# Decode attention, forward and backward over one KV cache: which cache blocks stay in SBUF between the four passes, and V turned in place at the end of the second pass

## The chip, the cores and the metric

The kernel runs on one core of a Trainium2 chip. The metric is device time in microseconds (us) from the start to the end of one execution, as a median over several. The core has TensorE (PE, matmuls and transposes by matmul), VectorE (DVE), ScalarE (ACT), GpSimd (POOL), SyncE (SP, which here issues every load), 16 DMA engines, the on-chip memories SBUF and PSUM, and HBM, which holds the inputs and outputs.

## The reference

Two transformer layers for one new token are computed with the same weights and the same KV cache, and then the gradient of everything, by `jax.vjp`:

```python
def A(x):      # attention, 32 query heads, 4 KV heads of 65536 keys x 128
    q = (x @ wq).reshape(32, 128)
    s = einsum("hd,hkd->hk", q, k) * 128 ** -0.5
    return (einsum("hk,hkd->hd", softmax(s), v)).reshape(4096) @ wo
def B(x):      # dense, squared relu, 1024 -> 3584 -> 1024
    return relu(x @ w1 + b1) ** 2 @ w2 + b2
x1 = x  + A(layernorm(x));   x2 = x1 + B(layernorm(x1))
x3 = x2 + A(layernorm(x2));  x4 = x3 + B(layernorm(x3))
outputs: x4 and the gradients of x, k, v, wq, wo, w1, b1, w2, b2
```

K and V have 4 groups x 65536 rows x 128 numbers in bf16: 64 MB (MiB) each, much more than SBUF holds. Each must be read again for every attention pass over it.

## The kernel before

**Four passes.** The cache is swept four times: p=0 is the forward attention of the first layer, p=1 that of the second, p=2 the backward pass of the second layer as far as it needs V and K for the gradient of q, p=3 the backward pass of both layers that also writes the gradients of K and V. Between them stand dense stages (`dense12` between p=0 and p=1, `dense23`, `dense34`), which stream the weights wo, w1, w2, wq.

**Steps.** A pass is a software pipeline of 256 items, each a group g (0 to 3) and 8 chunks of 128 rows; the 32 chunks that make a *block* of 1 MB in SBUF are four consecutive steps. A group has 16 blocks; K12 below is block 12 of the group at hand. In p=0 and p=1 (`attn_fwd`) an item goes through `kT` (lag 0: 8 transposes of K on PE into PSUM, one copy of 128x1024 on DVE or ACT back to SBUF), `kS` (lag 2: 8 matmuls for the scores) and `v8` (lag FWD_LAG: 8 matmuls for the output). Between `kS` and `v8` lie a chain of small steps (maximum, `turn`, `spread`, then the exponentials of a unit of 16 steps on ACT, line 996). In p=2 (`attn_bwd3`) V is transposed first (`vT`, lag 0; `vS`, lag 2) and K is read with lag 13 (`k8`); p=3 (`attn_bwd4`) does the same with blocks in falling order and K at lag 7, and stages its results, 1 MB per block, in SBUF before POOL issues the stores. The order on PE, DVE and ACT is the program's order in p=0 to p=2 (`manual_schedule`, lines 1059 and 1157); in p=3 the framework's scheduler sets it.

**Orders.** p=0 goes up through groups and blocks, p=1 goes down by units of 4 blocks but up inside a unit (first K12, K13, K14, K15, then K8 to K11 of group 3), p=2 goes up, p=3 goes down block by block.

**Slots.** All loads, kept blocks and staged results share an arena of 20 slots of 1 MB (`ARENA`, lines 240 to 246). Eight of them turn into planes for the exponentials as the passes go on (`hold`), so that 15 are left in the tail of p=0 and 12 from the end of p=1 on. `kv8` (line 320) loads a block, or two at once as 2 MB, where the program first touches it; `take_one` picks the slot. SP issues the loads in program order: it runs ahead of the engines until a load's slot is not yet free, and then everything behind that load waits too, the weights of the next dense stage among them.

**Keeping.** At the end of a pass up to `NKEEP` = 8, 7, 7 blocks are not given back but stay for the next pass. `TOUCH[p]` lists the blocks of a pass by first touch. `plan_keep` (line 382) takes, of the last NKEEP+2 blocks touched in pass p, those that the next pass touches first. That gives: after p=0, K15, V12, V13, V14, V15, V8, V9, V10 of group 3; after p=1, V0 to V6 of group 0; after p=2, K12, K13, K14, K15, V13, V14, V15 of group 3.

**Turned blocks.** A kept block whose transpose the pass makes anyway is overwritten by its transpose (`turned_to`, line 338: K in p=0, V in p=2). The next pass then skips `kT` or the 8 transposes and the copy of `vT` for it (`is_turned`). In p=1 K is what is transposed and V is what is kept, so nothing is turned there.

Of the kernel before, what the change touches and what calls it, by code (L numbers as in the profile page):

```python
# [20 lines left out]
def kernel(  # L21
# [24 lines left out]
    nc = tc.nc  # L46
# [10 lines left out]
    J = 32  # L57
    NB = C // J
    SU = min(128, C)
# [6 lines left out]
    TLEAD = 2  # L66
# [4 lines left out]
    NKEEP = [8, 7, 7]  # L71
# [16 lines left out]
    def ps_tr(shape=None, dtype=BF):  # L88
        return PS["pool"].tile(shape or [P, 8, P], dtype, name="ps_tr", tag="tr", bufs=2 if PS["pass4"] else 3)
# [7 lines left out]
    def ps_acc(shape):  # L97
        return PS["pool"].tile(shape, F32, name="ps_acc", tag="acc", bufs=1)
# [12 lines left out]
    ident_b = const.tile([P, P], BF, name="ident_b")  # L111
# [27 lines left out]
    def evac(out, in_, kind="bf"):  # L139
        n = 1  # L140
        for d in in_.shape[1:]:
            n *= d
        ca = 0.17 + n * 0.00083
        cd = 0.13 + n * (0.00105 if kind == "f32" else 0.00054)

        if PS["pass4"] and kind == "bf":
            ca += 1.5
        if kind == "kta" or kind != "kt" and load["act"] + ca <= load["dve"] + cd:
            load["act"] += 0.17 + n * 0.00083
            nc.scalar.copy(out=out, in_=in_)  # L150
        else:
            load["dve"] += cd
            nc.vector.tensor_copy(out=out, in_=in_)  # L153
# [161 lines left out]
    KV = {"have": {}, "keep": set(), "halves": set(), "turn": None, "turned": set()}  # L315
# [4 lines left out]
    def kv8(t, g, c8):  # L320
        hb, j = divmod(c8, J)
        key = (t, g, hb)
        have = KV["have"]
        if key not in have:
            i = None
            if NOW["pairs"] and hb % 2 == 0 and (t, g, hb + 1) not in have and key not in KV["halves"]:
                i = take_pair()
            if i is None:
                sl = Slot("blk_" + t, load=True)
                nc.sync.dma_start(out=sl.t.rearrange("p (j d) -> p j d", d=DH), in_=half(KVIN[t], g, hb))  # L330
                have[key] = sl
            else:
                for h in range(2):
                    have[(t, g, hb + h)] = Slot("blk_" + t, at=i + h)
                nc.sync.dma_start(out=wide(i).rearrange("p (j d) -> p j d", d=DH), in_=KVIN[t][g][hb // 2])
        return have[key].t.rearrange("p (j d) -> p j d", d=DH)[:, j:j + 8, :]
# [9 lines left out]
    def kv_done(t, g, c8):  # L346

        key = (t, g, c8 // J)
        if c8 % J == J - 8 and key not in KV["keep"]:
            KV["have"].pop(key).free()  # L350

    def order_by_unit(desc, unit):
        out = []
        gs = range(G)
        us = range(C // unit)
        for g in (reversed(gs) if desc else gs):
            for u in (reversed(us) if desc else us):
                out += [(g, c8) for c8 in range(u * unit, (u + 1) * unit, 8)]
        return out

    def touch_order(items, stages):
        seen, out = set(), []
        maxlag = max(l for _, l in stages)
        for i in range(len(items) + maxlag):
            for t, lag in stages:
                if 0 <= i - lag < len(items):
                    g, c8 = items[i - lag]
                    key = (t, g, c8 // J)
                    if key not in seen:
                        seen.add(key)  # L370
                        out.append(key)
        return out

    FWD_LAG = TLEAD + SU // 8 + 11
    B3_LAG = TLEAD + HB // 8 + 3
    B4_LAG = TLEAD + J // 8 + 1
    DV_LAG = TLEAD + 1
    ITEMS = [order_by_unit(False, SU), order_by_unit(True, SU), order_by_unit(False, HB), order_by_unit(True, J)]
    TOUCH = [touch_order(ITEMS[0], [("k", 0), ("v", FWD_LAG)]), touch_order(ITEMS[1], [("k", 0), ("v", FWD_LAG)]),
             touch_order(ITEMS[2], [("v", 0), ("k", B3_LAG)]), touch_order(ITEMS[3], [("v", 0), ("k", B4_LAG)])]  # L380

    def plan_keep(p):
        if p == 3:
            return set()
        last = TOUCH[p][-(NKEEP[p] + 2):]
        return set([k for k in TOUCH[p + 1] if k in last][:NKEEP[p]])

    def start_pass(p):  # L390
        KV["keep"] = plan_keep(p)
        KV["turned"] = KV.get("next", set())
        KV["next"] = set()
        KV["turn"] = {0: "k", 2: "v"}.get(p)
        NOW["pairs"] = p < 3
        KV["halves"] = set(TOUCH[p][-8:] + (TOUCH[p][:10] if p else []))
# [368 lines left out]
    def first_at(n, fn):  # L765
        TASKS.setdefault(NOW["i"] + n - 0.5, []).append(fn)
# [5 lines left out]
    def pipeline(items, stages, bg, end=(), holds=()):  # L772
        maxlag = max(l for _, l in stages)
        for i in range(len(items) + maxlag):
            NOW["i"] = i
            NOW["wide"] = NOW["pairs"]
            for at, k in holds:
                if i == at:
                    hold(k)
            tasks(i - 0.5)  # L780
            for n, (fn, lag) in enumerate(stages):
                if 0 <= i - lag < len(items):
                    fn(*items[i - lag])
                if n == 0:
                    tasks(i)
            bg.step(i)
            NOW["wide"] = False
            NOW["step"] += 1
            for before, fn in end:
                if i == len(items) + maxlag - before:  # L790
                    fn()
        while TASKS:
            k = min(TASKS)
            NOW["i"] = int(k + 0.5)
            tasks(k)
# [17 lines left out]
    def E(lay, g, c0, n):  # L813
        assert plane(lay, g) in HELD and plane(lay, g) not in BUSY
        return EALL[:, lay, g, c0:c0 + n, :]
# [73 lines left out]
    def attn_fwd(p, L, on_group, bg, end=()):  # L889
# [112 lines left out]
        def v8(g, c8):  # L1002
            su = c8 // SU
            vb8 = kv8("v", g, c8)
            if c8 % SU == 0:
                state["ps_o"] = ps_acc([P, 8, R])
            if c8 % SU == SU // 2 and su != first_su[g]:
                t = tmp.tile([P, R], F32, name="o_t")
                nc.vector.tensor_tensor(out=t[:], in0=state[("o", g)][:], in1=state[("al", g, su)][:], op=ALU.mult)
                state[("ot", g)] = t  # L1010
            ps_o = state["ps_o"]
            for i in range(8):
                c = c8 + i
                w = min(8, (su + 1) * SU - c)
                nc.tensor.matmul(ps_o[:, 0:w, :], lhsT=vb8[:, i, :], rhs=E(p, g, c, w),  # L1015
                                 start=(c % SU == 0), stop=(c % SU == SU - 1), skip_group_check=True)
            kv_done("v", g, c8)
            if (c8 + 8) % SU == 0:
                first_at(1, lambda: unit_end(g, su, ps_o))

        def unit_end(g, su, ps_o):
            on = spool.tile([P, R], F32, name="oacc", tag="oacc", bufs=3)
            rs = state.pop(("rs", g, su))
            if su == first_su[g]:
                nc.vector.tensor_copy(out=on[:], in_=ps_o[:, 0, :])
                z2 = rs
            else:
                al = state.pop(("al", g, su))
                nc.vector.tensor_tensor(out=on[:], in0=ps_o[:, 0, :], in1=state.pop(("ot", g))[:], op=ALU.add)
                zn = spool.tile([P, R], F32, name="zn", tag="zn")  # L1030
                nc.vector.tensor_tensor(out=zn[:], in0=state[("z", g)][:], in1=al[:], op=ALU.mult)
                z2 = spool.tile([P, R], F32, name="z2", tag="z2", bufs=3)
                nc.vector.tensor_tensor(out=z2[:], in0=zn[:], in1=rs[:], op=ALU.add)
            state[("o", g)] = on
            state[("z", g)] = z2
            if su == last_su[g]:
                after(2, lambda: group_sum(g, z2))
                after(3, lambda: group_out(g, su, on))
# [12 lines left out]
            nc.scalar.activation(out=L["fw"][:, g, :, :], in_=fd[:], func=ACTF.Exp)  # L1051

        start_pass(p)
        n = len(items) // G
        order = list(dict.fromkeys(g for g, _ in items))
        holds = [(k * n + 2, plane(p, g)) for k, g in enumerate(order) if k > 0]
# [2 lines left out]
        with tc.manual_schedule(engines=ORDERED):  # L1059
            pipeline(items, [(kT, 0), (kS, TLEAD), (v8, FWD_LAG)], bg, end, holds)  # L1060
        st.close()
# [381 lines left out]
    def on1(g):  # L1443
        if g != lastg[0]:
            bg.add(g_wo(L1, x1, g))
    attn_fwd(0, L1, on1, bg, [(10, pre_load("wo1", lambda: wo_slabs(lastg[0], 2)))])
    bg.drain()

# [190 lines left out]
```

## Time and profile before

| | |
|---|---|
| time, median of 4 runs | 2033.01 us (2031.31, 2032.86, 2033.15, 2041.23) |
| the profiled execution | 2041.23 us, span of the trace 2039.5 us |
| PE busy / DVE busy / ACT busy | 1656.6 / 1195.2 / 1048.3 us |
| bytes moved by DMA | 802.36 MB, 393 GB/s over the span |
| granted TensorE clock, mean | 0.896 of full speed |

One profiled execution is shown; it is the slowest of the four, 8.2 us above the median. A busy PE means that a matmul is in flight, not that the array is full. The tables by windows give, for each stretch of time, the busy time of each engine with its number of instructions, the granted clock, the share of time that the 16 DMA engines were busy (1.00 is all of it, rounding can give a little more) and the rate they moved.

By the first and last instructions of their lines, p=0 computes to 376 us, dense12 runs to about 427, p=1 to about 777, dense23 to 831, p=2 to 1198, dense34 to about 1250, p=3 to about 2015.

### The profile page before, as it was taken

The numbers are of one execution on the slowest core, as the hardware profiler recorded it, in microseconds if no ns is written. First come the engines' busy times: TensorE is split into PE (matmuls) and PEld (weight loads), VectorE is DVE, ScalarE is ACT, GpSimd is POOL, SyncE is SP. The second block draws the span as 40 slices with busy tenths as digits, with TensorE's granted clock in tenths as the row PEclk, the third lists the DMA queues.
The fourth block names the chain that finished last, engine by engine and source line by source line (L and its number), as shares of the span: only waits on it lengthen the run. The fifth ranks groups of instructions, "written<-read, shape, count | busy, mean of one in ns | idle before, by whom it ended". The sixth has DMA issues, their size and how long they took to land. (4 is left out here: it accounts for less than half of the span.)

```text
span 2039.5 us, 67934 instructions
## 1 busy us (share of the span) xinstructions
PE 1656.6 (81%) x30626; PEld 1364.1 (67%) x30626; DVE 1195.2 (59%) x2391; ACT 1048.3 (51%) x1620; POOL 144.2 (7%) x328
## 2 busy tenths in 40 slices
PE   6878788788887887877778788889788798698896
PEld 6878787788787776876667786555455455455554
DVE  5545464356554542535544457677658586677685
ACT  2434344244433433425444446777658585577575
POOL 0000000000000000000000001111112121111121
PEclk9989898699998986998998899989879897798898
DMA  9999999979999998899999996999999999999996
GB/s 389 424 416 419 421 422 412 358 299 389 419 419 415 418 414 313 343 419 413 424 416 419 414 364 236 419 424 422 416 408 409 359 423 403 371 408 423 424 376 254
DMA packets 112416, 802.36 MB, mean 393 GB/s; under 512 B 9584, under 2 KB 9598, under 8 KB 49534
## 3 DMA queue, kind: packets, MB, share of 16 engines
q1 hardware_dynamic: 88078, 632.33, 76.2%
q0 software_dynamic: 24048, 165.70, 19.6%
q8 instruction: 239, 3.92, 0.8%
q14 instruction: 51, 0.42, 0.1%
HBM read 632.30 MB, written 165.69 MB: 391 GB/s over the span
## 5 line engine op out<-in xcount | busy, mean ns | idle before, releaser
L153 DVE COPY kt<-ps_tr 128x1024 bf16<-128x1024 bf16 x809 | 555.5, 689 | 537.0 <-PE ps_tr L913 284.3
L150 ACT CAST arena<-ps_gg 128x1024 bf16<-128x1024 f32 (+2 forms) x455 | 442.6, 1009 | 200.3 <-PE ps_gg L1273 145.3
L913 PE MATMUL ps_tr<-ident_b,arena 128*128 128x128 bf16 x4064 | 332.3, 228 | 45.6 <-DMA arena<-in_A_k_cache_dram 31.4
L150 ACT COPY kt<-ps_tr 128x1024 bf16<-128x1024 bf16 x183 | 192.1, 1050 | 255.2 <-PE ps_tr L1098 160.1
L913 PEld LDWEIGHTS <-arena 128*128 128x128 bf16 x4064 | 251.0, 102 | 53.4 <-DMA arena<-in_A_k_cache_dram 34.7
L1015 PE MATMUL ps_acc<-arena 128*128 128x64 bf16 (+4 forms) x4096 | 212.6, 199 | 73.4 <-ACT arena L996 37.7
L153 DVE CAST arena<-ps_gg 128x1024 bf16<-128x1024 f32 (+2 forms) x188 | 225.0, 1197 | 65.7 <-PE ps_gg L1273 41.4
L1273 PE MATMUL ps_gg<-GG,xt 64*128 64x512 bf16 x1024 | 211.8, 412 | 40.1 <-DVE arena L153 20.7
L1219 PE MATMUL ps_tr<-ident_b,arena 128*128 128x128 bf16 x1952 | 188.8, 234 | 42.6 <-DMA arena<-in_A_v_cache_dram 40.9
L1015 PEld LDWEIGHTS <-arena 128*128 128x128 bf16 x4096 | 167.8, 103 | 76.2 <-issue 51.1
L931 PE MATMUL ps_sc<-L_qpad,kt 128*128 128x64 bf16 x4032 | 208.6, 196 | 7.0 <-issue 6.4
L1098 PE MATMUL ps_tr<-ident_b,arena 128*128 128x128 bf16 x2048 | 166.4, 227 | 39.8 <-DMA arena<-in_A_v_cache_dram 39.7
L1219 PEld LDWEIGHTS <-arena 128*128 128x128 bf16 x1952 | 127.3, 104 | 102.0 <-issue 55.9
L996 ACT ACTIVATE arena<-S_sb,L_negm 128x128 bf16<-128x128 f32 x256 | 164.5, 1002 | 49.9 <-DVE L_negm L981 49.9
L931 PEld LDWEIGHTS <-kt 128*128 128x128 bf16 x4032 | 175.7, 101 | 9.9 <-issue 6.6
L1098 PEld LDWEIGHTS <-arena 128*128 128x128 bf16 x2048 | 125.8, 102 | 43.8 <-DMA arena<-in_A_v_cache_dram 42.2
L1299 PE MATMUL ps_acc<-X,arena 128*128 128x64 bf16 (+3 forms) x2048 | 117.4, 198 | 13.4 <-DMA arena<-in_A_k_cache_dram 13.4
L996 ACT ACTIVATION_READ_ACCUMULATOR arena<-S_sb,L_negm 128x1 f32 x256 | 127.5, 498 | 0.0
L1252 PE MATMUL ps_sc<-DOB,kt 128*128 128x64 bf16 (+3 forms) x1952 | 125.1, 199 | 0.0
L1252 PEld LDWEIGHTS <-kt 128*128 128x128 bf16 x1952 | 90.7, 102 | 51.3 <-issue 50.0
L1299 PEld LDWEIGHTS <-arena 128*128 128x128 bf16 x2048 | 85.6, 101 | 45.9 <-issue 30.8
L1273 PEld LDWEIGHTS <-xt 64*128 64x128 bf16 x1024 | 61.1, 94 | 81.6 <-issue 42.3
(262 smaller groups left out, 2074.2 us busy)
## 6 DMA issues: line engine op xcount, KB each, us to landing
arena<-in_A_k_cache_dram SPq DMA_DIRECT2D x86, 2048.0 KB, 19.9
arena<-in_A_v_cache_dram SPq DMA_DIRECT2D x79, 2048.0 KB, 20.1
out_dram<-arena POOLq DMA_DIRECT2D x151, 1024.0 KB, 11.7
arena<-in_A_v_cache_dram SPq DMA_DIRECT2D x81, 1024.0 KB, 16.6
arena<-in_A_k_cache_dram SPq DMA_DIRECT2D x79, 1024.0 KB, 18.4
arena<-in_B_w_dram SPq DMA_DIRECT2D x32, 896.0 KB, 7.9
arena<-in_B_w_dram SPq DMA_DIRECT2D x21, 1024.0 KB, 9.9
arena<-in_A_wq_dram SPq DMA_DIRECT2D x20, 1024.0 KB, 16.2
```

Of the source, the lines that this page charges most:

```text
L150: nc.scalar.copy(out=out, in_=in_)
L153: nc.vector.tensor_copy(out=out, in_=in_)
L913: nc.tensor.transpose(pt[:, i, :], kb8[:, i, :], ident_b[:, :])
L931: nc.tensor.matmul(state["ps_s"][:, s:s + w, :].rearrange("p a b -> p (a b)"), lhsT=kt[:, i, :], rhs=L["qpad"][:, g, 0:w, :].rearrange("p ...
L996: nc.scalar.activation(out=E(p, g, c0, SU)[:, :, h], in_=S[:, h, :], func=ACTF.Exp, bias=L["negm"][:, g, su, h:h + 1], scale=SCALE, accum_ ...
L1015: nc.tensor.matmul(ps_o[:, 0:w, :], lhsT=vb8[:, i, :], rhs=E(p, g, c, w), start=(c % SU == 0), stop=(c % SU == SU - 1), skip_group_check=True)
L1098: nc.tensor.transpose(pt[:, i, :], vb8[:, i, :], ident_b[:, :])
L1219: nc.tensor.transpose(pt[:, i, :], vb8[:, i, :], ident_b[:, :])
L1252: nc.tensor.matmul(state["ps_dp"][:, s:s + w, :].rearrange("p a b -> p (a b)"), lhsT=vt[:, i, :], rhs=DOB[:, g, 0:w, :].rearrange("p a b - ...
L1273: nc.tensor.matmul(pg[:, 512 * h:512 * h + 512], lhsT=xt[64 * h:64 * h + 64, j1 // 8 + m, :], rhs=gg[64 * h:64 * h + 64, :, :].rearrange(" ...
L1299: nc.tensor.matmul(ps_dq[:, 0:w, :].rearrange("p a b -> p (a b)"), lhsT=kb8[:, i, :], rhs=X[:, s:s + w, :].rearrange("p a b -> p (a b)"), ...
```

## The change

```diff
-    FWD_LAG = TLEAD + SU // 8 + 11
+    FWD_LAG = TLEAD + SU // 8 + 12
...
     def plan_keep(p):
         if p == 3:
             return set()
-        last = TOUCH[p][-(NKEEP[p] + 2):]
-        return set([k for k in TOUCH[p + 1] if k in last][:NKEEP[p]])
+        return set([k for k in TOUCH[p + 1] if k[0] == "kvv"[p]][:NKEEP[p]])
...
             kv_done("v", g, c8)
+            if p == 1 and ("v", g, c8 // J) in early_turn:
+                pt = ps_tr()
+                for i in range(8):
+                    nc.tensor.transpose(pt[:, i, :], vb8[:, i, :], ident_b[:, :])
+                evac(vb8[:, :, :], pt[:, :, :], kind="kt" if c8 // 8 % 2 else "kta")
+                KV["next"].add(("v", g, c8))
...
         start_pass(p)
+        early_turn = set(k for k in TOUCH[p][:-2] if k in KV["keep"])
```

`plan_keep` now takes the first NKEEP blocks of one kind in the order of the next pass: K after p=0, V after p=1 and after p=2. That makes the kept sets K8 to K15 of group 3 after p=0 (one K and seven V before), V0 to V6 of group 0 after p=1 (the same set as before), V9 to V15 of group 3 after p=2 (three V and four K before). The number of kept blocks, and so the number of loads, is what it was. K kept in p=0 and V kept in p=2 are overwritten by their transposes through `turned_to`, which is unchanged.

In p=1, `v8` now transposes a kept V block right after its 8 matmuls and copies the result over the block, on DVE for every second item and on ACT for the others (`kind="kta"`). `early_turn` leaves out the last two blocks that p=1 touches, V2 and V3, so five blocks are turned: V0, V1, V4, V5, V6.

`FWD_LAG` is one step longer, 30 instead of 29 steps between `kT` and `v8`, in p=0 and in p=1.

## The prediction, made before the changed kernel was run

> **What bounds the kernel now.** I read the page's slices first, then windows of 5 us at the three dense stages, then PE's and SP's timelines there.
>
> ```profile
> DMA  9999999979999998899999996999999999999996
> GB/s 389 424 416 419 421 422 412 358 299 389 419 419 415 418 414 313 343 419 413 424 416 419 414 364 236 419 424 422 416 408 409 359 423 403 371 408 423 424 376 254
> ```
>
> Inside the passes the DMA engines are never free: 413 to 424 GB/s in most slices. At 420 GB/s a 1 MB block (1.049 MB decimal) costs 2.5 us. The bytes don't change with the edit, so inside a pass a faster engine is worth nothing. What can be won is DMA idle time, and that lies at the changes of pass: slices 8 and 9, 16 and 17, 24 and 25. There:
>
> ```profile
> core 0: us, PE busy (x) PEld busy (x) DVE busy (x) ACT busy (x) POOL busy (x), PEclk, DMA share, GB/s
> 425.00:462.50 37.50, 32.87 (x700) 32.22 (x701) 21.11 (x39) 12.42 (x25) 0.00 (x0) 0.91 0.60 228
> 775.00:795.00 20.00, 13.59 (x242) 13.03 (x242) 2.68 (x17) 1.77 (x3) 0.29 (x1) 0.64 0.65 239
> 840.00:860.00 20.00, 18.71 (x489) 17.95 (x486) 9.38 (x14) 7.35 (x8) 0.00 (x0) 1.00 0.71 258
> 1247.00:1270.00 23.00, 21.37 (x312) 13.85 (x310) 17.13 (x44) 14.15 (x16) 5.30 (x11) 0.85 0.26 104
> ```
>
> Against a share of 1.01 these are (1.01-0.60) x 37.5 = 15.4 us idle at the head of p=1, 7.2 us in the tail of p=1 and the layer norm behind it, 6.0 us at the head of p=2, 17.3 us at the head of p=3. The head of p=1 in detail, with SP's issues:
>
> ```profile
> 445.00:450.00 5.00, 4.45 (x108) 4.24 (x106) 3.81 (x8) 1.84 (x4) 0.00 (x0) 1.00 0.72 285
> 450.00:455.00 5.00, 1.80 (x45) 1.70 (x43) 1.37 (x2) 5.00 (x18) 0.00 (x0) 1.00 0.02 5
> 455.00:460.00 5.00, 5.00 (x103) 5.00 (x103) 1.97 (x3) 1.80 (x2) 0.00 (x0) 0.66 0.01 3
> ...
> 442.19 0.33 SPq L330 DMA_DIRECT2D arena<-in_A_v_cache_dram  x1
> 461.30 5.59 SPq L335 DMA_DIRECT2D arena<-in_A_k_cache_dram  x3
> ```
>
> Between 442 and 461 us SP issues nothing: seven slots hold V blocks that `v8` reads only from step 29 on, the rest hold K that is loaded and waits for its turn.
>
> **The change part by part.** The sum is made against the profiled execution (2041.2 us) and carried over to the median (2033.0) as a difference.
>
> *1. Head of p=1.* PE is rid of 28 groups of 8 transposes (7 more K blocks turned, 4 steps each). At full clock a step of `kT` and `kS` alone is 0.68 us apart, of which `kS` is 0.23:
>
> ```profile
> 440.67 0.35 PE L931 MATMUL ps_sc<-L_qpad,arena 128*128 128x64 bf16 x8
> 440.88 0.61 PE L913 MATMUL ps_tr<-ident_b,arena 128*128 128x128 bf16 x8
> 441.32 0.40 PE L931 MATMUL ps_sc<-L_qpad,kt 128*128 128x64 bf16 x8
> ```
>
> So a group of transposes costs PE 0.45 us. That is not the gain; the slots are. Before, nothing is given back until K blocks come in and are used. After, the first 32 steps of K need no load at all, so K12 can be used at once and frees its slot at step 5, K13 at 9, and so on, one per 4 steps. Following `take_one`, the loads stand in SP's order as wq, wq, V12, K4, V13, K5 (six slots that dense12's weights give back), V14-15 (K12 and K13's slots, step 9), K6-7 (step 17), V8-9 (step 25), K0-1 (step 33). From about 427 us the six keep the DMA busy 15 us, to 442, the three pairs 5 us each, to 457. Step 33 needs one chain of exponentials: some 7 us for the first 17 steps, 6 us for the small steps, 5 us for the exponentials (the ACT 5.00 above), 2 us more: 447. Each slot is free before the DMA gets to it, so the 15.4 us of idle go. Bounds: -15.4 (all) to -4 (the pairs come 11 us late, as when every one of the three waits 4 us, the length of one exponential wait). I take -14.5; PE's work is far below the DMA's pace.
>
> *2. Tail of p=0, and the lag.* Eight slots are held from step 224 on, so seven rotate for V. Before, V14, V15 and five w1 slabs were all issued by 364.75 us and shared the DMA:
>
> ```profile
> 369.90 1.89 PE L1015 MATMUL ps_acc<-arena 128*128 128x64 bf16 x32 [0.90 <-DMA arena<-in_A_v_cache_dram]
> 372.39 1.72 PE L1015 MATMUL ps_acc<-arena 128*128 128x64 bf16 x32 [0.60 <-DMA arena<-in_A_v_cache_dram]
> ```
>
> After, w1's first slab waits for V11 (`v8` through with it at 361.5 us), the next four for V12 to V15, one per some 1.9 us; the DMA needs 2.2 us for each and has V14 and V15 to do first. It should not run dry. Bounds: -1.5 (the two waits shown go, since w1 no longer competes) to +11 (five slabs x 2.2 us all come after the tail). One step more of lag costs 8 matmuls, 0.23 to 0.45 us, in each forward pass; its cover, the DMA, is absent only in the tail. I take +0.5 together.
>
> *3. Tail of p=1.* 20 groups (V0, V1, V4, V5, V6) are added where PE's order is the program's: 160 transposes, 20 copies, ten on DVE (0.69 us), ten on ACT (1.05 us). The tail before:
>
> ```profile
> 763.84 1.53 PE L1015 MATMUL ps_acc<-arena 128*128 128x64 bf16 x48
> 769.34 5.20 PE L1015 MATMUL ps_acc<-arena 128*128 128x64 bf16 x96 [3.97 <-ACT arena L996]
> 775.51 1.06 PE L1015 MATMUL ps_acc<-arena 128*128 128x64 bf16 x32 [0.98 <-DMA arena<-in_A_v_cache_dram]
> ```
>
> Twelve groups (V4 to V6) stand before the wait for the exponentials, among the small steps (`turn` at step 260, `spread` at 263): three groups before the last `kS` (1.35 us), about two behind `turn` that the chain does not cover (1.1), copies on DVE and ACT ahead of the small steps and between the exponentials (some 2 us: one of 0.69, one or two of 1.05): 4.5 us. Queued behind them on ACT are the eight exponentials, and for those waits `v8` of V0. Eight groups (V0, V1) come after: 8 x 0.45 = 3.6 us at full clock, less the 0.98 us wait for V3. That gives 7 us; at the clock granted here (0.60 for 770 to 775) a group is nearer 0.8 us (458.13 to 458.94 for a group at the low clock), 2.8 us more, of which I take a small part: +7.5. It costs in full: the slots are used up, w1's fourth slab waits for wo to be consumed, and the DMA already idles there. Bounds: 0 (all in the waits shown, 3.97 + 0.98 + 1.08 for `pmn`) to +20 (20 x 0.81 = 16.2, and four copies on ACT, 4.2).
>
> The Trainium skill, "TensorE: Matmul & The Clock Gate", section on the HAM clock gate, speaks against this part: after an idle window of some 3.4 us the array runs at half clock until it was busy for another. The granted clock of 0.60 behind a wait of 3.97 us agrees. By that rule alone all eight late groups would run at half speed and the term would be some 3 us larger, an estimate from that page.
>
> *4. Head of p=2.* The same 20 groups are gone from p=2, whose PE is full there (18.71 of 20 us). SP waits for V4 and V5 to give a pair of slots (issue at 857.24, step 23). Turned blocks are given back at `vS`, 2 steps later than at `vT`, so step 25 now, after 18 fewer groups: 18 x 0.45 less two steps of 1.1 us, about 6 us earlier. Idle to win there: 6.0. Bounds -6 to 0; I take -5.
>
> *5. Tail of p=2 and dense34.* V9 to V15 are held from step 228 on, five slots are left. By the slot order K14 waits for K11, K15 for K12, three w2 slabs for K13, K14, K15; before, all were free by step 252. The DMA has two wq blocks (5 us) between K13 and K14, so that I find no gap. Bounds 0 to +7.5 (three slabs x 2.5); I take 0.
>
> *6. Head of p=3.* Before, K12 to K15 lay in SBUF and V12, V11 were loaded; now V lies there and K15, K14 are loaded. The third load waits in both for V13 to be used:
>
> ```profile
> 1269.77 1.43 SPq L330 DMA_DIRECT2D arena<-in_A_v_cache_dram  x2
> 1276.16 0.33 SPq L330 DMA_DIRECT2D arena<-in_A_k_cache_dram  x1
> ```
>
> so the 17 us of idle stay. But what loads then is needed sooner: V8 and V10, for steps 28 and 20, become K12 and K13, for 19 and 15. Step 15's `k8` runs at 1276.28; K13, issued at 1270, shares the DMA with K12 and two stores, 4 MB or 10 us, and lands near 1278 to 1280. PE loses 2 to 4 us there, while 16 groups fewer (16 x 0.45 = 7 us) are on it by step 28. One load falls behind a store (2.5 us). Bounds -7 (PE is the bound, the groups count in full) to +9 (a store at 13.1 us and a load at 10.5 to land, 24 us, where 7 steps at 2.1 give 15). I take +1.5.
>
> Sum: -14.5 + 0.5 + 7.5 - 5 + 0 + 1.5 = -10 us: 2031 for the profiled execution, **2023 us** for the median.
>
> **The rivals.**
> *A, the forecast*: idle at p=1 wins, the tail of p=1 gives some back; own range 2014 to 2032. Chance 0.50.
> *B, the slots only move the gap*: the tail of p=0 starves instead (+11 of part 2 in place of +0.5): 2023 + 10.5 = 2033.5, no change. For it: the DMA share falls to 0.51 at 375 to 380 already, because slots are used up. Against it: each of the slots is freed one by one, in the order of need. Chance 0.17.
> *C, slower: K comes late in p=3*. Place: steps 15 to 27, K13, K11 and K10, each behind a store on a slot. Price: up to 9 us each, 27 at most, where p=3 can't catch up since PE and DMA are both near full (a DMA share of 0.97 to 1.02). At 27 in place of 1.5: 2048.5. It decides from 11.5 us on (no gain left), two of the three late. For it: 44.5 us of SP's waiting at 1244 to 1330 are for stores. Against: SP's third and fourth load keep their times. Chance 0.18.
> *D, more than forecast*: the added groups disappear in the waits of the tail (part 3 at 0, part 6 at 0): 2023 - 9 = 2014; own range 2010 to 2017. Chance 0.15.
> That the change does nothing is true of one part: the set kept after p=1 is the same, only its turning is new.
>
> **How the numbers follow.** The likeliest is A: 2023. The range goes down to D's middle less 2 and up to where C has lost the sum but not all: 2012 to 2042; outside lie a third of D, and of C what is above 2042, under 0.2. About 0.5% (10.2 us) is what a measurement can tell from no change. Faster than 2022.8: half of A (0.26 with its lower half) and D, 0.41. Within: 0.23 of A, 0.13 of B, 0.03 of C, 0.39. Slower: 0.15 of C, 0.05 of B and A, 0.20.
>
> **What would show it.** Right: the DMA share at 425 to 465 us stays near 1.0, and p=1 ends some 14 us earlier against the end of dense12; the idle time between p=1 and w1's stream grows by 5 to 10 us; the dip at the head of p=2 is gone. Wrong: a dip before dense12 longer than the 2.5 us at 375 to 380 (B); PE waits for in_A_k_cache at `k8` in the first 60 us of p=3 of more than 10 us in sum (C); a tail of p=1 as long as before (D).

## The result, and the profile after

| | before | after |
|---|---|---|
| median of the runs made beside each other | 2034.66 us (78 runs) | 2039.09 us (51 runs, 2030.95 to 2046.29) |
| ratio after to before | | 1.0019, 95% interval 1.0012 to 1.0025 |
| the profiled execution | 2041.23 us | 2035.27 us, span 2033.5 us |

The change makes the kernel slower by 0.19%, 3.9 us (0.0019 x 2034.66), less than the 0.5% named in the prediction as what can be told from no change, but with these many runs its interval leaves no change out. The forecast was 10 us faster; 2039.1 lies in the range of 2012 to 2042. Mind the profiles: before's is from the top of its runs and after's from the lower half, so the two traces differ by 6 us in the wrong direction. Stages can be compared, totals can't.

The page of after, its 40 slices:

```profile
DMA  9999999999999997999999996999999999999996
GB/s 390 423 416 421 420 422 406 368 359 421 419 419 402 420 415 274 369 418 411 423 417 420 411 354 245 344 419 424 421 420 423 374 424 398 374 412 425 424 394 244
```

Slices are counted from 0. The 7 of slice 8, with the head of p=1 in it, is a 9 (359 GB/s, 299 before); the gap behind p=1, slice 15, has grown (7 and 274 GB/s, before 8 and 313); slice 24, the head of p=3, is as it was. By windows, with columns as before: the head of p=1, the end of p=1 with the head of dense23, the head of p=2, the head of p=3.

```profile
425.00:462.50 37.50, 31.37 (x733) 30.61 (x732) 14.28 (x34) 14.61 (x39) 0.00 (x0) 0.82 0.87 348
765.00:785.00 20.00, 16.13 (x369) 15.68 (x367) 5.52 (x22) 5.59 (x7) 0.29 (x1) 0.84 0.48 171
840.00:860.00 20.00, 13.20 (x292) 12.72 (x291) 2.24 (x4) 2.02 (x2) 0.00 (x0) 0.74 0.74 299
1245.00:1270.00 25.00, 20.53 (x292) 12.48 (x291) 20.11 (x41) 15.81 (x17) 5.25 (x10) 0.91 0.56 203
```

Idle DMA time is (1.01 - share) x length. Head of p=1: 5.3 us (15.4 before). End of p=1: 10.6 us in these 20 us (7.2 before in 775 to 795). Head of p=2: 5.4 us (6.0 before): no gain. Head of p=3: 11.3 us in these 25 us, which begin later against p=3's first `vS` than the window of before does. So 10 us are won in the first, 3 to 4 given back in the second.

The lengths of the stages, each from the first or last instruction of its lines in one trace (us). The dense stages differ by up to 6 us from one execution to another even where the programs are the same (dense12 of e1 and of e10 below), so only larger or repeated differences count:

| stage | before | after | e1 | e3 | e7 |
|---|---|---|---|---|---|
| dense12, from `v8`'s end in p=0 to p=1's first `kS` | 57.7 | 56.4 | 49.9 | 54.1 | 53.6 |
| p=1, first `kS` to first `v8` | 23.2 | 14.4 | 14.6 | 24.3 | 14.4 |
| p=1, first to last `v8` | 321.6 | 327.2 | 319.5 | 322.5 | 327.1 |
| dense23, to p=2's first `vS` | 58.1 | 54.4 | 56.9 | 58.4 | 55.1 |
| p=2, first `vS` to first `k8` | 10.8 | 8.2 | 9.4 | 9.2 | 8.3 |
| p=3, first `vS` to last `k8` | 762.5 | 763.4 | 759.7 | 768.9 | 758.9 |

(e1: K kept after p=0 alone; e3: V kept after p=2 alone; e7: the change without V kept after p=2.) With K kept, p=1 reaches its first `v8` some 9 us sooner; with the turning, its `v8` takes some 5 to 8 us longer; the kernel that keeps V alone has the longest p=3.

The tail of p=1, PE's timeline of after (start, duration, instructions, and in brackets the idle time before with what ended it):

```profile
757.41 1.05 PE L1012 MATMUL ps_acc<-arena 128*128 128x64 bf16 x32
763.29 0.58 PE L1012 MATMUL ps_acc<-arena 128*128 128x64 bf16 x8 [4.83 <-ACT arena L993]
763.69 1.04 PE L1018 MATMUL ps_tr<-ident_b,arena 128*128 128x128 bf16 x8
...
773.71 3.73 PE L473 MATMUL ps_mv<-L_oTb,arena 128*128 128x64 bf16 x64 [0.70 <-DVE L_oTb L1049]
```

The wait for the exponentials is 4.83 us where it was 3.97: ACT has a copy of turned V among them. Then eight groups of transposes (line 1018) stand between the steps of `v8`. The last row is wo's first matmuls: 3.73 us here, 6.51 before.

The head of p=2, SP's issues of after:

```profile
833.28 0.33 SPq L330 DMA_DIRECT2D arena<-in_A_v_cache_dram  x1
845.75 0.33 SPq L335 DMA_DIRECT2D arena<-in_A_k_cache_dram  x1
```

For 12.5 us SP still issues nothing, because a pair of slots is not yet free.

The head of p=3, PE's table of waits at 1235 to 1345 us (total, times, longest) for after:

```profile
PE ps_tr L1223 <- DMA arena<-in_A_v_cache_dram: 9.7, 2, 7.5
PE ps_acc L1303 <- DMA arena<-in_A_k_cache_dram: 7.0, 1, 7.0
```

SP's of after:

```profile
SPq L330 <- DMA out_dram<-arena: 67.0, 11, 13.0
SPq L330 <- PE ps_sc L1256: 34.7, 3, 24.9
```

PE's for before:

```profile
PE ps_tr L1219 <- DMA arena<-in_A_v_cache_dram: 4.6, 1, 4.6
PE ps_acc L1299 <- DMA arena<-in_A_k_cache_dram: 2.2, 1, 2.2
```

SP's of before:

```profile
SPq L330 <- DMA out_dram<-arena: 54.4, 12, 6.4
```

In this window `k8` waits 7.0 us for one K block where it waited 2.2, `vT` 9.7 us for V in two waits where it waited 4.6 in one, and SP waits 12.6 us more for stores to give a slot back. Which K block it is, SP's timeline of after says:

```profile
1258.42 0.33 SPq L330 DMA_DIRECT2D arena<-in_A_k_cache_dram  x1
```

and PE's:

```profile
1273.46 1.03 PE L1303 MATMUL ps_acc<-X,arena 128*128 128x64 bf16 x16 [7.04 <-DMA arena<-in_A_k_cache_dram]
1301.41 1.04 PE L1223 MATMUL ps_tr<-ident_b,arena 128*128 128x128 bf16 x8 [7.48 <-DMA arena<-in_A_v_cache_dram]
```

K15 and K14 were issued in dense34; the load at 1258.42 is K13. It waited 24.9 us for `vS` (line 1256) to be through with a kept V block, and `k8` of K13 starts 15 us after the issue, when it lands. In between it shares the DMA with stores that POOL issues at 1257.63, 1259.51, 1261.28 and 1266.14. The second row is the first V block that this pass has to load, V8: SP issues it only at 1281.55, behind K12, K11 and K10, and PE waits 7.48 us for it.

### The profile page after: what moved, and what is told of

The parts are those of the page before. It is cut to its first block, busy times and chain, and to the rows that moved or that the text cites. A ratio compares the mean times of both kernels' runs of the same rounds, so it can differ in the third digit from the quotient of the medians.

```text
span 2033.5 us, 67140 instructions
## 1 busy us (share of the span) xinstructions
PE 1642.0 (81%) x30274; PEld 1343.7 (66%) x30274; DVE 1176.6 (58%) x2355; ACT 1043.0 (51%) x1612; POOL 144.2 (7%) x328
## 5 line engine op out<-in xcount | busy, mean ns | idle before, releaser
L153 DVE COPY kt<-ps_tr 128x1024 bf16<-128x1024 bf16 x722 | 496.2, 689 | 451.0 <-PE ps_tr L910 225.6
L150 ACT CAST arena<-ps_gg 128x1024 bf16<-128x1024 f32 x452 | 440.3, 1009 | 218.5 <-PE ps_gg L1277 168.4
L910 PE MATMUL ps_tr<-ident_b,arena 128*128 128x128 bf16 x3840 | 311.3, 227 | 61.4 <-DMA arena<-in_A_k_cache_dram 50.0
L150 ACT COPY kt<-ps_tr 128x1024 bf16<-128x1024 bf16 x162 | 169.5, 1046 | 218.2 <-PE ps_tr L1102 154.0
L910 PEld LDWEIGHTS <-arena 128*128 128x128 bf16 x3840 | 234.6, 101 | 65.7 <-DMA arena<-in_A_k_cache_dram 53.3
L153 DVE CAST arena<-ps_gg 128x1024 bf16<-128x1024 f32 (+1 forms) x191 | 228.8, 1198 | 74.5 <-PE ps_gg L1277 37.5
L1223 PE MATMUL ps_tr<-ident_b,arena 128*128 128x128 bf16 x1824 | 180.3, 237 | 36.0 <-DMA arena<-in_A_v_cache_dram 35.1
L1012 PEld LDWEIGHTS <-arena 128*128 128x128 bf16 x4096 | 163.6, 101 | 58.7 <-issue 41.1
L928 PE MATMUL ps_sc<-L_qpad,kt 128*128 128x64 bf16 (+7 forms) x3584 | 184.4, 194 | 17.0 <-issue 16.8
L1102 PE MATMUL ps_tr<-ident_b,arena 128*128 128x128 bf16 x1888 | 157.6, 231 | 41.0 <-DMA arena<-in_A_v_cache_dram 39.3
L1223 PEld LDWEIGHTS <-arena 128*128 128x128 bf16 x1824 | 121.5, 106 | 92.2 <-issue 52.2
L928 PEld LDWEIGHTS <-kt 128*128 128x128 bf16 x3584 | 154.0, 100 | 19.9 <-issue 17.7
L1102 PEld LDWEIGHTS <-arena 128*128 128x128 bf16 x1888 | 119.8, 104 | 44.8 <-DMA arena<-in_A_v_cache_dram 41.6
L1303 PEld LDWEIGHTS <-arena 128*128 128x128 bf16 x2048 | 87.3, 102 | 52.2 <-issue 33.4
L1256 PEld LDWEIGHTS <-kt 128*128 128x128 bf16 x1824 | 86.7, 103 | 50.1 <-issue 48.6
L1256 PE MATMUL ps_sc<-DOB,kt 128*128 128x64 bf16 (+3 forms) x1824 | 119.3, 201 | 0.0
L1147 PE MATMUL ps_acc<-dsT,arena 128*128 128x64 bf16 (+7 forms) x2048 | 104.5, 196 | 18.1 <-DMA arena<-in_A_k_cache_dram 14.4
```

The costliest lines, as they stand in the source:

```text
L910: nc.tensor.transpose(pt[:, i, :], kb8[:, i, :], ident_b[:, :])
L928: nc.tensor.matmul(state["ps_s"][:, s:s + w, :].rearrange("p a b -> p (a b)"), lhsT=kt[:, i, :], rhs=L["qpad"][:, g, 0:w, :].rearrange("p ...
L1102: nc.tensor.transpose(pt[:, i, :], vb8[:, i, :], ident_b[:, :])
L1147: nc.tensor.matmul(ps_dq[:, 0:w, :].rearrange("p a b -> p (a b)"), lhsT=kb8[:, i, :], rhs=dsT[:, s:s + w, :].rearrange("p a b -> p (a b)") ...
L1223: nc.tensor.transpose(pt[:, i, :], vb8[:, i, :], ident_b[:, :])
L1256: nc.tensor.matmul(state["ps_dp"][:, s:s + w, :].rearrange("p a b -> p (a b)"), lhsT=vt[:, i, :], rhs=DOB[:, g, 0:w, :].rearrange("p a b - ...
```

## The experiments

All medians are us; the last column is (ratio - 1) x the median of before beside it.

| run | edit against before | median | ratio, 95% interval | us |
|---|---|---|---|---|
| e1 | K8 to K15 kept after p=0 | 2024.84 | 0.9951 (0.9939 to 0.9963) | -10.0 |
| e2 | V0, V1, V4 to V6 turned in p=1 | 2037.76 | 1.0011 (1.0000 to 1.0022) | +2.2 |
| e3 | V9 to V15 kept after p=2 | 2046.77 | 1.0063 (1.0051 to 1.0075) | +12.8 |
| e4 | one step more of lag | 2038.59 | 1.0021 (1.0010 to 1.0031) | +4.3 |
| e5 | e1 + lag | 2030.26 | 0.9982 (0.9968 to 0.9997) | -3.7 |
| e6 | e1 + turning | 2029.22 | 0.9973 (0.9956 to 0.9990) | -5.5 |
| e7 | the change without V kept after p=2 | 2029.48 | 0.9977 (0.9963 to 0.9990) | -4.7 |
| e8 | e3, K15, K14, K13 loaded at p=3's first step | 2036.51 | 1.0014 (0.9999 to 1.0030) | +2.8 |
| e9 | e1 + lag in p=0 alone | 2028.26 | 0.9964 (0.9952 to 0.9976) | -7.3 |
| e10 | e1 + lag in p=1 alone | 2031.92 | 0.9970 (0.9956 to 0.9985) | -6.1 |
| e11 | e1, one step less | 2025.42 | 0.9946 (0.9934 to 0.9958) | -11.0 |
| e12 | e1, three steps more | 2025.31 | 0.9948 (0.9933 to 0.9962) | -10.6 |
| e13 | e1 again | 2025.64 | 0.9947 (0.9927 to 0.9967) | -10.8 |
| e14 | e1, TensorE kept busy in p=0's tail | 2024.47 | 0.9939 (0.9922 to 0.9956) | -12.4 |
| e15 | e5, the same | 2026.16 | 0.9948 (0.9928 to 0.9967) | -10.6 |
| e16 | e14, and in p=1's tail | 2022.86 | 0.9939 (0.9925 to 0.9953) | -12.4 |
| e17 | the whole change, TensorE kept busy in p=0's tail | 2035.54 | 1.0003 (0.9989 to 1.0017) | +0.6 |
| e18 | e7, the same | 2026.71 | 0.9955 (0.9937 to 0.9973) | -9.2 |

**One part at a time (e1 to e4).** e1 and e3 put the new `plan_keep` in for one pass, e2 only the turning, e4 only the lag:

```diff
     def plan_keep(p):
         if p == 3:
             return set()
+        if p in (0,):        # e1; (2,) in e3
+            return set([k for k in TOUCH[p + 1] if k[0] == "kvv"[p]][:NKEEP[p]])
         last = TOUCH[p][-(NKEEP[p] + 2):]
```

> The kernel before, with only the blocks kept after p=0 changed (K8 to K15 of group 3 in place of one K and seven V). Theory 1 (the idle DMA at the head of p=1 is won and stays won): about 10 us faster, ratio 0.995, the DMA idle time between 425 and 465 us falls from 15.6 to about 5 us. Rival (what is won at the head of p=1 is lost again before the end of p=1 or in the tail of p=0, since the slots stay the same): within 2 us of before, ratio 0.999 to 1.001, with the head as full as in theory 1.

> The kernel before, with only the turning of V0, V1, V4, V5, V6 at the end of p=1 added. Theory 1 (the tail is longer and the DMA idles longer there, the head of p=2 wins nothing back): 3 to 6 us slower, ratio 1.0015 to 1.003, idle DMA time between the end of p=1 and w1's stream up by 3 to 5 us, at the head of p=2 unchanged at about 5.6 us. Rival (the head of p=2 wins as much as the tail loses, as the prediction had it to within 2.5 us): ratio 0.999 to 1.001.

> The kernel before, with only the blocks kept after p=2 changed (V9 to V15 in place of V13 to V15 and K12 to K15). Theory 1 (K13 and the K blocks after it come late, behind stores, but p=3 catches up, since the DMA bounds it): 0 to 3 us slower, ratio 1.000 to 1.0015. Rival (rival C of the prediction in a small form: late K is not caught up, and this part holds the whole loss): 6 to 15 us slower, ratio 1.003 to 1.007.

> The kernel before, with only the longer lag of v8 (30 steps in place of 29). Theory 1: the waits of v8 for the exponentials get shorter, but the DMA bounds both forward passes: ratio 0.9995 to 1.0005. Rival (the other order of the V and K loads makes the passes or their tails slower): 2 us slower or more, ratio over 1.001.

One part wins 10 us, three cost: V kept after p=2 most by far. The four add up to +9.3 us where the whole has +3.9, so they overlap. e3's PE timeline shows the same wait for K13, 28.4 us behind p=3's first `vS` (28.8 in after; before, this block's `k8` ran at 23.7), and the one for V8 behind it:

```profile
1281.62 1.03 PE L1301 MATMUL ps_acc<-X,arena 128*128 128x64 bf16 x16 [6.77 <-DMA arena<-in_A_k_cache_dram]
1308.88 1.03 PE L1221 MATMUL ps_tr<-ident_b,arena 128*128 128x128 bf16 x8 [6.89 <-DMA arena<-in_A_v_cache_dram]
```

From p=3's first `vS`, `k8` of the sixth block comes at 46.5 us in e3 and 47.0 in after, 54.8 before: the wait for K13 is made up at once, since the turned V needs no transposes. Then comes the wait for V8, and `k8` of the eleventh block is late, at 122.7 us in e3 and 124.4 in after, 117.3 before; of the seventeenth at 194.0, 195.8 and 185.6 (184.7 to 189.3 in the traces that keep the old set). What is lost there is work of the DMA. The 50 us that begin 30 us after the first `vS`, of before, after and e3 (the last numbers are the DMA share and GB/s):

```profile
1282.60:1332.60 50.00, 40.83 (x534) 25.68 (x532) 32.40 (x53) 32.67 (x37) 8.78 (x17) 0.90 1.01 423
1274.70:1324.70 50.00, 41.04 (x466) 24.54 (x465) 28.76 (x44) 27.31 (x30) 8.01 (x15) 0.73 0.91 338
1283.20:1333.20 50.00, 41.52 (x472) 24.82 (x472) 29.74 (x45) 27.71 (x31) 8.73 (x17) 0.73 0.91 339
```

338 and 339 GB/s in place of 423 are 4.2 MB less, or 10 us at 423 GB/s. All 16 traces that keep the old set after p=2 have 423 or 424 in these 50 us.

**Pairs (e5 to e7).** On top of e1 the lag or the turning; and the whole change with the old set after p=2.

> K8 to K15 kept after p=0, and the longer lag; nothing turned in p=1, and the old set after p=2. Theory 1 (the parts add up, and the longer lag costs about 4 us wherever it stands): -9.9 + 4.2, ratio about 0.9972. Rival (the longer lag is what a head of p=1 without transposes wants, since v8 waited 3.67 us for the exponentials there in the changed kernel as well): ratio 0.995 or less.

> K8 to K15 kept after p=0, and five V blocks turned at the end of p=1; lag 29, the old set after p=2. Theory 1 (parts add up): -9.9 + 2.3, ratio about 0.9963. Rival (the turning is free once p=1 begins earlier, or wins at the head of p=2): ratio 0.995 or less.

> The changed kernel with the old set kept after p=2 (K12 to K15, V13 to V15), everything else as changed. Theory 1 (the V blocks kept for p=3 are the costliest part, in this company too): 8 to 13 us faster than the changed kernel, ratio to before 0.9955 to 0.998, p=3 from its first vS to its last k8 in 757 to 762 us. Rival (the part alone lost to a chance of the slot order, and not in the changed kernel): ratio to before 1.000 to 1.002.

On e1 the lag costs 6.3 us and the turning 4.5. Taking V's keeping out of the whole change wins 8.5 us (1.0019 - 0.9977): with it gone, the rest is faster than before. In the table of stages p=3 shows 4.5 us of that: 763.4 us in after, 758.9 in e7. One pair of traces can't tell it, since p=3 takes 757.5 to 765.8 us in the 16 traces with the old set; in after, e3 and e17 it takes 763.4, 768.9 and 770.5.

**Is the late load the reason? (e8)** The kept set of e3 stays; K15, K14 and K13 are asked for at the first step of p=3 instead of at their first use, so that SP issues them ahead of everything that waits for stores:

```diff
         def vT(g, c8):
             bg.need(g)
+            if (g, c8) == items[0]:
+                for b in (15, 14, 13):
+                    kv8("k", g, b * J)
             vb8 = kv8("v", g, c8)
```

> V9 to V15 kept after p=2 as in e3, and in addition the loads of K15, K14 and K13 issued at step 0 of p=3, so that all three take slots that dense34 gives back, and none waits for a store of p=3. Theory 1 (the loss of e3 starts with K13, whose slot first takes a staged result: block 2 of k8 28.5 us after the first vS in place of 22.6, and p=3 never makes it up): at least half of e3's 12.7 us goes, ratio 1.000 to 1.003, block 2 at 22 to 23 us. Rival (the loads are not later but too few slots are free, so that the wait goes to the staging or to K12): the ratio stays at 1.005 or more, with block 2 on time and a later block late.

10 of the 12.8 us go (the intervals leave 4 us either way). SP's timeline of e8 has the loads of K14 and K13 here:

```profile
1244.42 5.14 SPq L330 DMA_DIRECT2D arena<-in_A_k_cache_dram  x2
```

and e3's those of K13 and K12 here:

```profile
1266.85 4.75 SPq L330 DMA_DIRECT2D arena<-in_A_k_cache_dram  x2
```

In e8 K13 is out 8 us before p=3's first `vS` (1257.1), in e3 14 us after it (1253.2). K15 and K14 move by 1 us or so; the loads behind K13, down to V8, come out 2 to 5 us sooner. `k8` of the third block comes at 18.3 us instead of 28.5, the wait for V8 is 4.2 us instead of 6.9, the eleventh block's `k8` comes at 114.2 us instead of 122.7, and in the 50 us shown above for e3 the DMA moves 389 GB/s:

```profile
1287.10:1337.10 50.00, 36.31 (x411) 21.56 (x408) 26.84 (x44) 25.23 (x28) 7.53 (x15) 0.78 0.98 389
```

PE's waits for K at `k8` are not much shorter in sum (8.2 us, 9.7 in e3), and their first is now a later block's, at 1291.77. So most of the price of keeping V is the time at which these loads are issued, not the bytes (which are the same) and not the turned blocks. In e3 K13 waits for `vS` as in after, 25.3 us; stores are what the loads behind it wait for, and those loads moved with it.

**What is the lag's price? (e9 to e12)** `FWD_LAG` changed by pass and by size on e1's base: 30 in p=0 alone, in p=1 alone, 28 and 32 in both (29 before, 30 in the change).

> K kept after p=0 as in e1, and one step more of lag in p=0 alone. e5, with the step in both forward passes, cost 6 us more than e1. Theory T (the cost lies in the tail of p=0: v8 ends a step later there, the slots that w1's slabs wait for come free later, and dense12 starts late): about 2030, as e5, while e10 stays at 2025. Theory U (half in each pass, a step of matmuls and some waits at both tails): 2028 here and in e10. Theory V (the cost lies at the head of p=1, where V's first blocks are read one step later): 2025 here.

> K kept after p=0 as in e1, and one step more of lag in p=1 alone. T: 2025. U: 2028. V or a cost in the tail of p=1: 2030.

> K kept after p=0 as in e1, lag one step shorter than before (28) in both forward passes. If the step costs through its length (6 us a step, steadily), a step less gains: about 2019 to 2023. If 29 is a best point between waiting for exponentials and holding slots, v8 waits longer for the exponentials and it is no faster: 2025 to 2030.

> K kept after p=0 as in e1, lag three steps longer than before (32) in both forward passes. A steady price per step: 2043 (18 us more than e1). A price that falls once, because of where one step puts v8 against the exponentials and the slots: 2028 to 2034.

By e9 and e10 the step costs 2.7 and 3.9 us, together about e5's 6.3, as theory U has it, a part in each pass; but each of the two has an interval of 3 to 4 us. By e11 and e12 one step less gains nothing and three steps more cost nothing, which no theory had: what is paid is not a step's length. e10's twelve runs spread over 13 us, four at 2022 to 2025 and eight at 2030 to 2036. The traces give a lead. The window of 375 to 380 us, of e1:

```profile
375.00:380.00 5.00, 4.09 (x66) 3.85 (x65) 0.70 (x6) 1.51 (x2) 0.29 (x1) 1.00 1.01 417
```

of e10:

```profile
375.00:380.00 5.00, 4.30 (x43) 4.23 (x44) 0.67 (x5) 1.51 (x2) 0.29 (x1) 0.53 0.90 366
```

and of after:

```profile
375.00:380.00 5.00, 4.30 (x41) 4.23 (x41) 0.67 (x5) 1.51 (x2) 0.29 (x1) 0.50 0.81 310
```

e1 and e10 are the same program up to here, with granted clocks (third number from the end) of 1.00 and 0.53; dense12 lasts 49.9 and 56.0 us. Before has 0.50 as well.

**Is it the clock? (e13 to e18)** e13 is e1 once more. The others put transposes of the identity, which nobody reads, into the waits of p=0's tail (e16: p=1's too):

```diff
+        def warm(n):
+            pt = ps_tr()
+            for i in range(n):
+                nc.tensor.transpose(pt[:, i % 8, :], ident_b[:, :], ident_b[:, :])
+
         def v8(g, c8):
             su = c8 // SU
             vb8 = kv8("v", g, c8)
+            at = items.index((g, c8)) if p in (0,) else 0
+            if at == 240:
+                warm(40)
...
             kv_done("v", g, c8)
+            if at in (243, 247, 251, 255):
+                warm(12)
```

> The program of e1 once more, beside the next three. Clock theory: the same program gives dense12 at about 50 us or at about 56 us from one execution to the next; times about 2025, spread over 6 to 10 us.

> e1 with 88 transposes of the identity that nobody reads in the tail of p=0: 40 ahead of the last unit's v8 (whose wait for the exponentials is 3.98 us) and 12 behind each of its four blocks. Clock theory: the granted clock is 1.00 at 365 to 380 us, dense12 takes 50 us or less, 2020 to 2024 and a narrower spread. If the clock there is of no account: 2025 to 2027 (the added work, 88 x 0.057 = 5 us on PE, of which 1 or 2 lie on the path).

> e5 (K kept after p=0, one step more of lag) with the same 88 transposes. Clock theory: the lag's 6 us go, 2020 to 2025, within 1 us of e14. If the lag costs by slots or waits: 2028 to 2032, some 6 above e14.

> e14 with the same 88 transposes in the tail of p=1 too. There wo's 64 matmuls took 3.73 us in the trace of e1 and 6.51 us in the trace of before, and w1's first groups ran at 0.50 of the clock. Clock theory: 1 to 3 us less than e14. If the loads bind there (w1 is waited for at 772 to 779 us in e1): no change.

> The whole change with the 88 transposes of e15 in the tail of p=0. Clock theory: 4 us less than the changed kernel, 2035, even with before, and wo's 64 matmuls take 3.73 us. If the clock is of no account in it: 2038 to 2040.

> e7 (the whole change but for V kept after p=2) with the 88 transposes. If the two causes add: 8.5 us less than e17 and 4 less than e7, 2025 to 2027; what is left over e14 is then the turning's, 1 to 3 us. If e7 had the clock's cost out already: 2029.

The row of wo's first 64 matmuls in dense12, in PE's timeline of e1:

```profile
375.22 3.73 PE L478 MATMUL ps_mv<-L_oTb,arena 128*128 128x64 bf16 x64 [0.70 <-DVE L_oTb L1048]
```

of e13:

```profile
376.25 6.58 PE L478 MATMUL ps_mv<-L_oTb,arena 128*128 128x64 bf16 x64 [0.71 <-DVE L_oTb L1048]
```

and of e15:

```profile
375.76 3.73 PE L478 MATMUL ps_mv<-L_oTb,arena 128*128 128x64 bf16 x64 [0.71 <-DVE L_oTb L1058]
```

e1 and e13 are one program: 3.73 and 6.58 us. In the 15 traces without the added transposes wo took 3.73 us in two (e1, e11) and 5.01 to 6.58 in thirteen; with them it took 3.73 in all five. Dense12 is shorter on average where wo took 3.73, but the two groups overlap: 49.2 to 53.6 us (mean 51.8) in those seven traces, 52.2 to 57.7 (mean 55.2) in the thirteen. e14's dense12 took 51.4 us, where the expectation had 50 or less.

What the added transposes are worth differs: 1.6 us on e1 (e14 against e13, inside the intervals), 6.9 on e5 (e15), 3.3 on the whole change (e17), 4.5 on e7 (e18); the intervals on these differences are some 5, 5, 3 and 5 us either way, so that only the second and third are clear of them, the third barely. With TensorE kept busy the step of lag costs 1.8 us (e15 against e14, where 1 or less was expected) instead of 6.3, but with intervals of 5 and 4 us these two are not told apart. Nor do the traces tell the lags apart: without the added transposes wo is slow in all five with 30 steps in p=0, but also in seven of the eight with 29. That the lag costs through the clock is not shown.

Ahead of wo, a row of e5's PE timeline shows where the clock goes down:

```profile
369.91 1.66 PE L1017 MATMUL ps_acc<-arena 128*128 128x64 bf16 x32 [2.76 <-DMA arena<-in_A_v_cache_dram]
```

and its counterpart in e15, with 12 of the added transposes ahead of it and the next block behind it:

```profile
366.42 0.83 PE L1007 MATMUL ps_tr<-ident_b 128*128 128x128 bf16 x12
369.75 1.11 PE L1025 MATMUL ps_acc<-arena 128*128 128x64 bf16 x32 [2.50 <-DMA arena<-in_A_v_cache_dram]
372.25 1.72 PE L1025 MATMUL ps_acc<-arena 128*128 128x64 bf16 x32 [0.27 <-DMA arena<-in_A_v_cache_dram]
```

In e5 this block's 32 matmuls wait 2.76 us for their load and then run slowly (1.66 us); in e15 the wait is nearly as long and the matmuls take 1.11, but the next block's take 1.72: the clock goes down there too (0.66 in the mean at 370 to 375 us) and is back at 1.00 when wo starts. In e1's trace that wait is 0.44 us, in e13's 1.98: the wait itself moves from one execution to another.

e16 is the fastest of all, 2022.86, but its ratio is the same as e14's. In p=1's tail wo took 3.73 us in it and 5.36 in e13 and e14, but 3.73 in e1 too, the program of e13; and there is no gain that the intervals tell: the theory for that tail is not confirmed.

**The account.** Going from e1 to after by runs: -10.0 (e1), +0.8 to e18 (turning and lag come in, and the added transposes with them), +9.8 to e17 (V kept after p=2), +3.3 to after (the added transposes go), together +3.9. The sum closes by construction; that e17 and e18 came out at 2035.54 and 2026.71, where 2035 and 2025 to 2027 were written down before, does not.

## Why the prediction was wrong

*Part 1, head of p=1 (-14.5): right mechanism, smaller.* The load queue no longer stalls; 10 us of DMA idle time went, and e1 measures -10.0 in the time. The 5 us left, of which the forecast had 1, are in two pieces: the DMA share is 0.57 and 0.73 at 425 to 435 us, and 0.78 at 445 to 450, where `v8` waits for its exponentials.

*Part 2, tail of p=0 and the lag (+0.5): wrong on the lag.* The tail itself does not starve: e1, which has all of it, keeps its 10 us, and the DMA share at 375 to 380 us is 1.01 there and 0.81 in after, 0.51 before. Rival B is out. But the step of lag was priced by its eight matmuls and cost +4.3 (e4) and +6.3 (e5). Why it costs that much is open: with TensorE kept busy it came to 1.8 us, within intervals that don't tell this from 6.3. The prediction weighed in part 3 alone that PE's work after a wait can run at a lower clock; on wo's 64 matmuls in dense12 that is 1.3 to 2.9 us.

*Part 3, tail of p=1 (+7.5): right for the stage.* The stage is some 5 to 8 us longer wherever V is turned. In the time the turning costs 2.2 us (e2) or 4.5 (e6), since dense23 gives some back: 54.4 to 57.9 us in after, e2, e6 and e7, 56.5 to 58.7 in before, e1, e3, e4 and e5. Parts 3 and 4 together had the turning at +2.5, as e2 measured it alone, but by two misses that cancel, which is luck. The late groups at low clock, feared at 2.8 us more, worked the other way: the first two run at 1.04 us, the others at 0.61, and wo behind them takes 3.73 us instead of 6.51 (3.73 in all six traces with the turning, 3.73 to 6.58 in the others). The Trainium skill's rule ("TensorE: Matmul & The Clock Gate", section on the HAM clock gate) that an idle window halves the clock and a busy one restores it holds in these rows; it was applied to the added groups only, and not to what follows them.

*Part 4, head of p=2 (-5): missing.* 5.4 us of idle stay of 6.0. p=2 reaches its first `k8` 1 to 2.6 us sooner, but SP still waits for a pair of slots, 833.28 to 845.75; the gap has moved forward with the rest. The estimate of how early the slots come free was not met; by how much of it PE's lower clock there (0.74, before 1.00) is to blame was not tried.

*Part 5 (0): right, as far as one trace tells.* dense34 lasts 55.2 us, before 55.0 (53.8 to 60.3 over all the traces).

*Part 6, head of p=3 (+1.5): the step that failed.* It measured +8.5 (e7), +9.8 (e18 to e17), +12.8 alone (e3). The forecast saw K13 coming late, with PE losing 2 to 4 us, and counted on 16 groups fewer on PE to pay for it; of the loads behind K13 it had only one behind a store, at 2.5 us. In the run the wait for K13 is 7.0 us in after and 6.8 in e3, and it is paid back as forecast: `k8` of the sixth block is 8 us ahead of before. What had no term is the rest of the queue: six K loads stand in SP's order ahead of V8, four of them behind a slot that `vS` or a store has to give back. PE waits 7.5 us for V8 (6.9 in e3), and the DMA moves 338 GB/s in place of 423 from 30 to 80 us after the first `vS`. That is 10 us of DMA work, by an estimate from the two rates, and it does not come back: in the 120 us behind it the DMA share is 1.01 in before and after alike. In e8, where these loads come out sooner, the same estimate gives 4 us, and 2.8 were measured. The place was rival C's, but not its sign, waits for K of more than 10 us in the first 60 us: they are 7.0 us in after, and the second wait is for V.

*The sum.* Against its forecast part 1 fell short by 4.5 us, the lag by 4 to 6, the turning (parts 3 and 4) by 0 to 2, part 6 by 7 to 11. That is 15 to 24 us, with 14 measured (-10 to +3.9): the parts overlap, as the singles' +9.3 against +3.9 shows too. Had only part 6 been sized right, the forecast would have been within 3 us of no change.

Open: why one step of lag costs and three don't (e12's trace has wo at 6.54 us and the run is still at e1's time), and why the time behind p=3's last `k8` is 25.5 us in the kernels that keep V (25.3 in e3) and 24.2 to 24.4 in the others.

## What to carry to other kernels

Keep in SBUF what the next pass reads first only if what is displaced can be loaded before anything blocks the in-order load queue: after p=0 that held and gave 10 us, after p=2 the displaced K stood in the queue behind a block still in use and then behind stores, and its late loads, with the V loads behind them, cost about 10. A wait that the engine makes up can still hide a queue that runs dry: compare what the DMA moved in the stretch behind it. Price a wait not by its length alone but with the matmuls behind it, whose clock it can take down (wo: 5.0 to 6.6 us in place of 3.73). And test a bundle of edits one by one: here one edit of four was worth having, and alone it beats both kernels (2024.84 us).

## What the runs showed of the hardware

One program gave wo's 64 matmuls 3.73 us in e1 and 6.58 in e13, at a granted clock of 1.00 and 0.50 from 375 to 380 us; dense12 took 49.9 and 54.4 us (56.0 in e10, whose program is the same up to there). The Trainium skill's page "TensorE: Matmul & The Clock Gate" says, in the part on the HAM clock gate, that the activity window is free-running, so that it depends on where in the window work begins. The traces agree: in all 20 the granted clock alternates between 1.00 and 0.50 in stretches that are whole multiples of 3.41 us, and near 370 us one such stretch begins at 370.51 in e1, at 372.01 in e13.

A wait need not fill such a stretch to take the clock down. e5's wait of 2.76 us lies in the stretch from 366.80 to 370.22 us, in which PE was busy for 0.19 of the time; behind it the clock is at 0.50. Cut into pieces of 3.41 us along these stretches, the 20 traces have 518 at full clock with PE busy for less than 0.4 of the time, and half clock follows in all of them; from half clock to full it went only behind pieces with PE busy for 0.78 or more.

88 transposes that nobody reads, placed in waits, went with 3.73 us for wo in five traces of five, and cost nothing that could be measured (e14 against e13: 1.6 us faster, inside the intervals).
